# A new hand-out of places: the same 1,848 steps of a recurrence and four attention experts in another order

## The chip, the core and the metric

The kernel runs on one core of a Trainium2 chip. The engines are TensorE (PE in the profile, its weight loads PEld), VectorE (DVE), ScalarE (ACT), GpSimd (POOL) and SyncE (SP), which starts the DMAs. The metric is the device time of one execution in microseconds (us); of three executions of the kernel before, the median is 308.04 us (307.08 to 311.17).

## The reference

Two stages, with B=4 batches, H=8 heads, S=768 steps, D=48, and then E=4 experts with 64 columns each.

```python
for t in range(S):                       # stage 1: a recurrence over steps, per batch and head
    cur = einsum(u * k[t], v[t])
    y[t] = einsum(r[t], state + cur)
    state = w[t] * state + einsum(k[t], v[t])
x = y as (B, S, H*D)                     # (4, 768, 384)
logits = x @ w_gate                      # stage 2: the 2 best of 4 experts for each row
for e in range(4):
    q, k, v = x @ wq[e], x @ wk[e], x @ wv[e]
    a = softmax(causal(0.125 * q @ k.T))
    out += gate[e] * (a @ v @ wo[e])
```

## The kernel before

The 768 steps of a batch are cut into two halves of six chunks of 64 steps, so there are eight units (batch, half). Each unit goes through the recurrence (`rwkv`) and then through the experts (`moe`); different units overlap.

**Recurrence.** The heads go in pairs, two pairs together (in the first unit pair by pair). DVE scans the decays of a chunk (L623 backward, L630 forward), and keys and receptances are multiplied with the results (L632, L634, L636, L638, on DVE or POOL). PE turns the scaled keys (L257 as one 128x128 product, L261 as two products on quarters of the array: the first when the product ahead used the whole array), makes each chunk's state increment (L445) and the products inside a chunk (L686), whose copy is masked (L693). DVE carries the state from chunk to chunk, one step an instruction (L468, first step L470 or L472, last step L464). PE then adds both parts of the output into one bank (L399, L401: the output products), and DVE adds the bonus term (L412 in the first unit, where PE sums the bonus with L570). PE turns the sums into columns for the experts.

**Experts.** Projections (L772 and L811 in the first unit in plain fp32, L779 and L817 after it), scores (L881), row maximum and mask on DVE (L892), exponential on ACT (L897), transposes (L257, L261), a times v (L929), gates (L966, L978), output projection (L1000), copy and store.

**What sets the order.** Nothing is scheduled while the kernel runs or is built: every step was given a number when it was planned, and the table `ORDER` lists the numbers with the letter of an engine (A is ACT, V DVE, P PE, G POOL, S SP). The lists of the engines are followed one by one:

```python
listed = [(letters[x[0]], int(x[1:])) for x in ORDER.split()]
for e, n in listed:
    o = ops[n]                     # also picks the buffer and the bank that o gets
...
    o["fn"](o["how"])              # writes the instructions of o
    if e == "PE":  pe = ...        # the last product so far
    elif e == "SP" and pe is not None:
        tc.add_manual_dep(own, pe.name, ...)   # "pace": a DMA waits for it
```

So an entry's place sets its place in its engine's queue, and for a DMA also the product after which it may start. A step whose plan allows two engines goes to the one whose letter it has.

**Warming products.** 94 steps (numbers 8 to 101, line L1054) multiply a constant tile by itself and write a bank that nobody reads; a step that isn't in the table isn't made. They need only the constant and a free bank.

```python
for i in range(WARM[0] + WARM[1]):
    plan.add("warm", {"PE": 216}, lambda e, w=w: nc.tensor.matmul(w()[:, 0:512], wz[:, 0:128], wz, ...), [], [w], ...)
```

Other lines: L329 and L330 (`masks3`) make the mask inside a chunk, L333 (`masks2`) the causal mask, L563 the bonus products, L578 the products of two decays, L643, L656, L664 and L666 the bonus of later units, L267 and L265 copies on DVE and ACT.

Of the kernel before, what the change touches and what calls it, by code (L numbers as in the profile page):

```python
# [1095 lines left out]
A0 V4 S113 V123 V124 A1 V126 S114 S115 S116 A5 A125 V120 G128 S6 S117 P79 S176 P53 P28 P9 P68 P88 P10 G129 V3 S177 P94  # L1096
S180 S119 P21 V127 P86 V130 P34 P90 V145 V131 P133 P100 V146 V148 V149 P50 P20 G142 G150 V152 P27 G151 V147 V153 S243
S244 V2 P57 G184 A134 P135 V185 A136 S118 V137 S245 V187 P31 V138 P143 A144 P155 A156 P121 S178 V188 P47 P157 G154
A158 G206 V159 A122 G132 S246 V160 V139 V161 P165 S102 A168 G169 V207 V162 A208 S7 S107 V140 V163 V209 V141 V210 A251
A186 P164 V166 G250 V252 A274 V253 A268 P51 P173 V174 P170 S249 G255 G257 V171 P74 V254 S179 P237 A238 A295 V203 V181  # L1100
V211 P265 P204 V213 G212 V189 A266 P182 A183 V214 V191 A205 P216 G190 V192 G193 V256 A217 S287 G258 S288 A105 G106
P267 P218 A219 G294 V220 V269 V221 V222 P194 A195 P225 S289 P196 V227 A197 V198 G299 A108 V223 V199 V200 G300 V224
V201 S340 P226 V229 A103 V202 G104 V270 V275 P231 V276 V232 A215 P234 V235 V277 S248 S247 V271 G347 V278 V279 S293
V272 V273 S290 V296 V297 S342 V298 V348 P916 P241 P239 P280 V281 V259 V260 A240 A242 G301 S341 G302 V261 V263 G353
G352 V349 S291 G303 G304 V283 P912 P913 S384 G391 S386 A312 A318 S385 P920 P921 P922 A923 P914 A915 G354 P967 P917
P918 V350 V351 G397 A264 A919 P968 P969 P309 A970 A310 P937 P946 V938 A939 V940 A941 A262 V949 A950 V947 A948 P311
V319 V320 S343 V313 V314 V315 V316 P955 V956 A957 V317 V321 V322 V323 P944 A945 V305 V307 S344 A392 V393 V394 A306
P971 V958 P972 P973 A974 A308 P924 P925 P926 P324 P285 S292 P928 P929 V325 A959 P930 P951 V327 P953 S387 G355 V286
A927 S346 P960 A931 V932 A954 V396 A952 A961 V356 G357 G933 P362 P962 S438 P975 V976 A363 V978 A977 G398 V395 P331
S437 A332 G109 A963 A360 S439 V333 G444 P329 V330 P364 P942 V371 V943 P984 P337 V985 A365 P334 A335 A338 S345 V358  # L1110
A359 S388 V372 V373 A986 G399 S110 V336 V374 A361 S535 V339 A979 V375 V376 S390 V366 V987 A988 V367 V368 S480 V369
S482 V370 S481 P964 P965 P966 A1005 P377 V378 V380 V400 P1033 P1034 P1041 P1035 V448 V401 P1042 P1043 P1037 A1036
A1044 P980 P991 A981 A992 A934 V935 P1038 V402 A111 P1039 A1040 V404 S441 P993 P989 A990 G449 P982 A983 G405 V996 V994
P1058 A997 V1061 G936 P406 A407 V1059 V445 A995 V1007 V1008 G1009 V446 P1067 P1000 A1001 G1010 V1070 A1062 V1068 P408
A415 A409 V410 A403 V416 V411 G112 P1049 P998 A1060 A999 V417 V418 V419 V412 V413 V414 P1050 P1051 A1052 P1045 P1046
P1047 V447 P1011 P1091 P1092 A1012 A1071 G487 S440 A1048 G452 V420 P1093 A1094 G450 P1013 V1014 A1015 P421 V422 P1074
A1075 V424 P1076 V1077 P1065 A1066 A1069 A1078 V1079 A1080 G1016 P382 V383 V451 V488 V1053 V453 V491 V456 S533 G492
G1054 S532 G543 V454 V489 G539 P1002 S389 A461 P1003 P1004 A1006 S534 S484 S442 P458 A459 P1072 A1073 P1081 A1082
P1095 P1096 P1097 A1098 A467 P1017 V1018 A1019 G1020 P460 V462 V468 V463 V469 V464 V470 P473 V474 A476 P1083 A1084
A1055 A457 V471 V465 P1099 V1102 A1103 V1100 A1101 V472 A455 V466 P426 V427 A510 V490 S486 S443 P1108 G494 V1111 V1109  # L1120
A1112 V1056 V493 V495 V540 V496 S577 S483 G1057 V497 G477 G545 P1021 P1063 P434 P1104 A435 S575 A1064 P1022 A1023
S1024 G582 V541 S576 P1029 P1030 A1105 A504 P1025 P1026 A1027 S1028 A1031 S1032 A1110 P1117 V1118 P501 A502 V499 S536
G544 V1120 P1085 P428 A429 P431 V430 A432 V433 V436 P1086 P503 V505 V511 V512 V506 V513 V507 A1119 A1121 A498 V1134
V542 V514 V508 V515 V509 P478 V479 S485 G546 S629 P516 V517 V583 V587 A519 V547 S627 V586 V548 V549 V1135 S538 G520
G1136 V551 S628 A500 G588 S578 V584 G1137 P1087 G639 P1088 P1089 P1090 A1132 P1106 A1107 P1115 A1116 P553 A554 S579
P1160 P1161 P1162 A1163 V1164 P1165 P1166 P1167 A552 P555 V556 V557 G634 V558 V562 V559 V563 V564 V565 V560 A1168
V1169 V566 P568 A571 V569 V567 V561 A550 P521 V522 P1222 P1223 P1224 S580 A1225 V1226 V590 S537 V585 V589 P1113 P523
A524 V525 A1114 G572 P1124 S768 S670 P1217 P1218 G591 G638 P1138 A1125 S672 A1139 P1219 A1220 V1221 P529 A530 P1122
P596 A1123 V531 P1140 V1141 P1187 P1196 A597 P526 A1142 A527 P1205 V1190 V1188 V1197 A594 V1199 A1200 V528 A595 A1198
V635 G1143 A592 G677 A593 A1191 S671 G681 G640 A1189 P611 V612 P598 V605 V599 V600 V601 V602 V1206 S631 S630 V606 V636  # L1130
V607 V608 V609 V610 G682 A1207 P573 V574 V603 V604 P1126 V614 A651 V637 V641 S581 V678 V642 P1127 P1128 P1129 P1130
S633 P1131 A657 S722 A1133 P1303 P1304 P1305 V679 P1170 P1171 V643 P1295 P1172 P1299 A1306 P648 P1192 A1193 P1203
A1204 P1300 P1301 A649 A1173 A1302 V680 P1296 P1297 A1298 A644 V1307 G1308 P1144 A645 S723 G683 G729 V646 A647 V1145
A1146 A1309 P650 G1147 V1208 V658 V659 S674 S673 P663 A1209 V652 V660 V666 V664 V653 V654 P616 V617 P1178 P1179 P1180
P1290 P1291 P1345 V685 P1292 V686 A1181 P1346 A1293 A700 V1310 V687 P1347 A1348 P1174 V1349 P1175 P1176 V655 G684 A689
G690 S726 A1177 P621 P624 A694 S765 V661 V662 P1210 V656 G1311 A625 A622 S632 V1294 V626 A1211 V623 P1350 P1351 P1352
V1182 V730 G1183 A1353 V1354 A688 P1285 P1286 P1287 A1288 V1289 P1156 P1157 G733 G735 S823 P1194 A1195 A1158 P1227
V731 V1228 G772 P618 V1230 S724 G734 P1201 V1202 S767 P691 A619 P1236 P1245 V620 V1239 A1231 A692 V1237 P1212 A1213
V1248 P1234 A1235 V1246 A1247 S766 P693 S1159 V701 V695 V702 V696 V703 V697 V698 V699 V704 A1229 A1184 V1185 G1186
P668 V705 S675 V669 V732 A1238 A1249 A1240 V1259 G737 S725 G736 V1260 G1261 G738 G1262 P1214 P1215 P1216 P1250 A1251  # L1140
S819 P1252 G777 A1253 P1312 V1315 S817 G776 G829 S676 P1243 P1241 A1257 A1242 A1244 A1316 S818 V1313 A1314 P1148 P1149
# [126 lines left out]
```

## Time and profile before

| | us |
|---|---|
| three executions | 308.04, 307.08, 311.17 |
| the profiled execution | 308.01 |
| its span, first to last instruction | 306.1 |
| PE busy in the span | 295.6 |
| DVE busy | 248.1 |
| ACT, POOL busy | 222.0, 155.3 |
| mean granted clock of TensorE | 0.989 |

The span is what the trace shows; 1.91 us of the profiled execution lie around it. A matmul's end is modelled, so that products that follow each other closely overlap in the trace, and a short wait can hide in a busy time. The granted clock is told as a share of 2.4 GHz, so 0.50 is 1.2 GHz.

### The profile page before, as it was taken

The page shows a single profiled execution, that of the slowest core. Times are in us where ns is not written, and L with a number is a line of the kernel's source. Part 1 is how long each engine was busy: PE and PEld are TensorE (multiplying, and loading weights), DVE is VectorE, ACT ScalarE, POOL GpSimd, SP SyncE. Part 2 cuts the span into 40 slices and gives each one's busy share as a digit, 9 for nine tenths or more (in the row PEclk, how much of TensorE's full clock was granted, in tenths as well). Part 3 has the DMA queues.
Part 4 walks back from the last instruction along what each step waited for, and adds up shares of the span by engine and source line. Part 5 has one row for each costly group of instructions (what it writes and reads, how often), then busy time and mean ns, then how long its engine had stood idle before and what let it go on. Part 6 is the DMA issues. An engine that isn't in the chain of part 4 may idle for free.

```text
span 306.1 us, 12703 instructions
## 1 busy us (share of the span) xinstructions
PE 295.6 (97%) x5216; PEld 245.0 (80%) x5216; DVE 248.1 (81%) x703; ACT 222.0 (73%) x688; POOL 155.3 (51%) x247
## 2 busy tenths in 40 slices
PE   7879999899999999999999999999999999999995
PEld 2669669778886897999789778898889977898784
DVE  5987999989999999989898997978587644687652
ACT  4336399988999889889899867464788656649852
POOL 4848597928556548267787769634211101210510
PEclk9995999999999999999999999999999999999999
DMA  7976785881649763656671573010100000000212
GB/s 227 359 277 216 255 277 167 292 300 43 212 134 329 222 208 117 218 163 207 206 232 77 173 271 107 6 41 24 51 28 2 0 28 28 2 26 2 79 62 94
DMA packets 20073, 44.09 MB, mean 144 GB/s; under 512 B 2352, under 2 KB 10032, under 8 KB 20016
## 3 DMA queue, kind: packets, MB, share of 16 engines
q1 hardware_dynamic: 20016, 43.29, 42.8%
q8 instruction: 41, 0.67, 0.9%
q14 instruction: 16, 0.13, 0.1%
HBM read 38.56 MB, written 4.72 MB: 141 GB/s over the span
## 4 chain that ended last, share of the span: by engine, by line
PE 93%; DVE 3%; issue 1%; DMA 1%; SPq 0%; ACT 0%; DVEq 0%; ACTq 0%
PE ps L779 16%; PE ps L929 13%; PE ps L881 12%; PE ps L1000 9%; PE ps L261 9%; PE ps L817 8%; PE ps L686 5%; PE ps L257 4%; PE ps L399 4%; PE ps L401 4%; PE ps L445 3%; PE ps L772 3%; PE ps L811 1%; DMA lt<-in_wkr_dram 1%; PE ps L978 1%
## 5 line engine op out<-in xcount | busy, mean ns | idle before, releaser
L897 ACT ACTIVATE a<-a,mx 128x128 f32<-128x128 f32 (+5 forms) x96 | 63.8, 667 | 10.0 <-DVE mx L892 9.6
L892 DVE CUSTOM_DVE_ANT_0 a<-ps,causal 128x256 f32<-128x256 f32 (+5 forms) x96 | 56.4, 619 | 12.2 <-PE ps L881 10.8
L265 ACT COPY AT<-ps 128x512 f32<-128x512 f32 (+5 forms) x74 | 38.6, 546 | 10.1 <-PE ps L261 7.9
L929 PE MATMUL ps<-AT,v_sb 128*64 128x384 f32 (+2 forms) x308 | 40.4, 405 | 0.1
L468 DVE CUSTOM_DVE_ANT_0 ys<-ps,ys,suf 112x48 f32<-112x48 f32 x144 | 33.4, 262 | 3.2 <-PE ps L445 0.4
L929 PEld LDWEIGHTS ps<-AT,v_sb 128*64 128x64 f32 x308 | 20.0, 136 | 16.5 <-issue 12.2
L664 ACT ACTIVATE xn<-nat,rk 128x48 f32<-128x48 f32 x126 | 30.5, 326 | 2.0 <-DVE rk L656 1.9
L779 PE MATMUL ps<-xh,wh_qk 128*128 128x384 f32 x84 | 30.4, 362 | 0.0
L881 PE MATMUL ps<-K,Q 64*128 64x384 f32 (+4 forms) x160 | 30.2, 415 | 0.0
L779 PE MATMUL ps<-xl,wh_qk 128*128 128x384 f32 x84 | 28.4, 338 | 0.1
L779 PE MATMUL ps<-xh,wl_qk 128*128 128x384 f32 x84 | 28.3, 336 | 0.0
L989 POOL TENSOR_TENSOR yl<-yr,yh 128x384 fp32r<-128x384 f32 x13 | 13.1, 1010 | 27.5 <-ACT yh L988 26.3
L399 PE MATMUL ps<-vy,am 64*64 64x48 f32 x768 | 25.8, 225 | 1.3 <-issue 1.3
L261 PEld LDWEIGHTS ps<-ident,a 64*128 64x128 f32 x560 | 23.1, 138 | 4.4 <-issue 1.6
L261 PE MATMUL ps<-ident,a 64*128 64x64 f32 x560 | 26.3, 225 | 0.1
L401 PE MATMUL ps<-ys,pre 48*64 48x48 f32 x704 | 25.5, 224 | 0.0
L636 POOL TENSOR_TENSOR kt<-lt,suf 128x768 f32<-128x768 f32 x13 | 21.9, 1685 | 6.3 <-DVE kr L643 3.5
L401 PEld LDWEIGHTS ps<-ys,pre 48*64 48x64 f32 x704 | 22.9, 138 | 2.2 <-DVE wend L464 1.1
L399 PEld LDWEIGHTS ps<-vy,am 64*64 64x64 f32 x768 | 23.5, 139 | 0.1
L638 POOL TENSOR_TENSOR pre<-lt,w 128x768 f32<-128x768 f32 x11 | 18.6, 1690 | 9.6 <-DVE w L630 5.4
L686 PE MATMUL ps<-pre,kt 48*64 48x64 f32 x768 | 18.3, 227 | 1.4 <-issue 0.7
L693 DVE TENSOR_TENSOR am<-ps,dec_mask 64x384 f32<-64x384 f32 (+1 forms) x33 | 18.2, 552 | 1.4 <-PE ps L686 1.0
(173 smaller groups left out, 823.2 us busy)
## 6 DMA issues: line engine op xcount, KB each, us to landing
lt<-in_wkr_dram SPq DMA_DIRECT2D x28, 384.0 KB, 4.4
kr<-in_nat_dram SPq DMA_DIRECT2D x14, 576.0 KB, 4.2
lt<-in_wkr_dram SPq DMA_DIRECT2D x14, 397.0 KB, 4.4
nat<-in_nat_dram SPq DMA_DIRECT2D x16, 288.0 KB, 3.9
vy<-in_vY_dram SPq DMA_DIRECT2D x32, 144.0 KB, 3.7
out_dram<-ob SPq DMA_DIRECT2D x24, 192.0 KB, 1.9
lt<-in_wkr_dram SPq DMA_DIRECT2D x3, 583.0 KB, 5.8
w_qk<-in_wqk_dram SPq DMA_DIRECT2D x1, 768.0 KB, 8.0
```

The lines of the kernel that those rows point to most:

```text
L261: nc.tensor.transpose(o()[:, h * 512 + i * 64:h * 512 + i * 64 + 64], src[r], ident[r, r])
L265: nc.scalar.copy(o, i)
L399: nc.tensor.matmul(to, am()[k, c, :], vy()[k, c, :], start=zero and x == 0, stop=i == 2 and x == len(group) - 1)
L401: nc.tensor.matmul(to, pre()[r, c, :], ys()[r, c, :], start=i == x == 0, stop=False)
L468: nc.vector._custom_dve(TENSOR_TENSOR_REDUCE_ADD_MIN, out=new, in0=inc, in1=old, s0=3.0e38, s1=by)
L664: nc.scalar.mul(to[:, i, h, :], v()[:, i, h, :], rk()[:, i, h:h + 1])
L686: nc.tensor.matmul(apss[x]()[half(h if first else h ^ x), c * C:(c + 1) * C], kt()[r, c, :], pre()[r, c, :], start=True, stop=True)
L779: nc.tensor.matmul(pp()[:, 0:384], w[:, qk, k, cs], x()[:, k, :], start=(k == j == 0), stop=(k == j == 2))
L881: nc.tensor.matmul(spv(x)[:, h, :], q_()[p, t], flat(k_())[p, o], start=j == 0, stop=j == len(terms) - 1)
L892: nc.vector.tensor_tensor_reduce(out=a()[:, 0:n].rearrange("p (a n) -> p a n", a=np_), in0=spv(x), in1=causal[:, S - n:S].rearrange("p (a ...
L897: plan.add("exp", {"ACT": t_exp(n)}, lambda e, x=x, y=y, mx=mx, a=a: nc.scalar.activation(a()[:, 0:n], a()[:, 0:n], AF.Exp, bias=mx(), sca ...
L929: nc.tensor.matmul(yp()[e * 64:e * 64 + 64, lo:hi], v_sb()[:, j, ep * 128 + e * 64:ep * 128 + e * 64 + 64], at, start=(j == 0), stop=(j == ...
```

## The change

Only the table `ORDER` is another one. It lists 1,848 steps, where the one before has 1,847. 83 steps change the engine: 34 from ACT to DVE, 31 from DVE to ACT, 9 from POOL to DVE, 6 from DVE to POOL, 2 from POOL to ACT and 1 from ACT to POOL. Warming products: 22 in place of 21. The rows of the product lines stay in number, but for the transposes, of which 22 of quarters (L261) become 11 of the whole array (L257), because the product ahead of them is another one.

```diff
 ORDER = """
-A0 V4 S113 V123 V124 A1 V126 S114 S115 S116 A5 A125 V120 G128 S6 S117 P79 S176 P53 P28 P9 P68 P88 P10 G129 V3 S177 P94
...
+V4 S113 V123 A0 V2 A5 V3 S115 S114 S116 V124 V120 S6 V126 G128 P92 V127 G129 V130 S117 P54 S176 P53 P68 V145 V146 V148
...
 """
```

**PE, first pair of heads.** Before: the last state increments, all products inside the chunks, one warming product, and the output products:

```order
L445 MATMUL ps<-nat_129,kts_212 48x48 x12
L686 MATMUL ps<-pre_155,kt_150 64x64 x24
L1054 LDWEIGHTS causal
L1054 MATMUL ps<-causal 128x512
L401 MATMUL ps<-ys_234,pre_155 64x48 x2
L399 MATMUL ps<-vy_145,am_260 64x48 x4
```

Now (the lines left out are three more warming products):

```order
L445 MATMUL ps<-nat_134,kts_204 48x48 x12
L686 MATMUL ps<-pre_143,kt_132 64x64 x12
L1054 LDWEIGHTS causal
L1054 MATMUL ps<-causal 128x512
...
L686 MATMUL ps<-pre_143,kt_132 64x64 x12
L401 MATMUL ps<-ys_227,pre_143 64x48 x2
```

The products of the two heads' chunks are parted, and four warming products stand between them. Ahead of the first keys' transposes stand eight warming products where there were twelve; up to the end of the output products there are 18 in place of 20, and nothing else is more or less there.

**PE, behind the output products of the first pair.** Before:

```order
L399 MATMUL ps<-vy_197,am_289 64x48 x4
L1054 LDWEIGHTS causal
L1054 MATMUL ps<-causal 128x512
L257 MATMUL ps<-ident,xn_323 128x128 x3
L257 MATMUL ps<-ident,kt_350 128x128 x6
L570 MATMUL ps<-u_t,kr_363 128x2 x6
L257 MATMUL ps<-ident,kt_376 128x128 x3
```

Now (left out: two more warming products):

```order
L399 MATMUL ps<-vy_192,am_284 64x48 x4
L1054 LDWEIGHTS causal
L1054 MATMUL ps<-causal 128x512
...
L257 MATMUL ps<-ident,xn_316 128x128 x3
L257 MATMUL ps<-ident,kt_319 128x128 x6
L1054 LDWEIGHTS causal
L1054 MATMUL ps<-causal 128x512
L570 MATMUL ps<-u_t,kr_349 128x2 x6
```

Three warming products stand where one stood, and a fourth ahead of the bonus sums. The first projection step (L772) goes ahead of the second pair's last products inside chunks, and the next unit's products inside chunks (L686, 24 rows) go ahead of two transposes of the sums.

**DVE, the start.** Before, the mask (L329, L330) stands behind both heads' scans; the rows here are the first after the constants:

```order
L578 TENSOR_TENSOR w_114<-lt_66 128x199
L623 SCALAR_TENSOR_TENSOR ps<-w_114,ps 128x198
L628 RECIPROCAL ps<-ps 128x6
L563 TENSOR_TENSOR kr_125<-lt_66 128x2x192
L333 TENSOR_SCALAR causal<-d_78 128x128
L630 SCALAR_TENSOR_TENSOR ps<-w_114,ps 128x198
...
L329 TENSOR_SCALAR dec_mask<-d_78 64x64
```

Now:

```order
L578 TENSOR_TENSOR w_112<-lt_66 128x199
L329 TENSOR_SCALAR dec_mask<-d_78 64x64
L330 TENSOR_SCALAR dec_mask<-d_78 64x64
L333 TENSOR_SCALAR causal<-d_78 128x128
L623 SCALAR_TENSOR_TENSOR ps<-w_112,ps 128x198
L563 TENSOR_TENSOR kr_124<-lt_66 128x2x192
L628 RECIPROCAL ps<-ps 128x6
```

Both masks now stand ahead of the bonus product (L563), which needs two loads. Further on, the next unit's receptance product (L634, 128x384) leaves DVE for POOL, and six state steps (L468) of the next unit that stood behind the second pair's additions (L412) stand ahead of them. The loads keep their set; the weights of the projections (`w_qk`) start four loads earlier.

## Rows read from the trace of the kernel before

**Rows 1.** The page, busy time of each engine, share, instructions.

```profile
PE 295.6 (97%) x5216; PEld 245.0 (80%) x5216; DVE 248.1 (81%) x703; ACT 222.0 (73%) x688; POOL 155.3 (51%) x247
```

**Rows 2.** Stretches: us, length, each engine's busy us (instructions), granted clock, DMA share, GB/s.

```profile
6.60:23.66 17.06, 13.25 (x302) 10.47 (x303) 15.71 (x43) 5.88 (x19) 11.35 (x16) 1.00 0.87 310
23.66:30.48 6.82, 6.64 (x168) 6.27 (x168) 4.77 (x19) 4.00 (x12) 5.62 (x5) 0.50 0.75 241
30.48:298.00 267.52, 265.93 (x4709) 222.80 (x4711) 222.62 (x629) 207.13 (x647) 135.53 (x214) 1.00 0.40 131
```

**Rows 3.** PE's waits up to 31 us: line, for whom, us in total, times, longest.

```profile
PE ps L399 <- issue: 1.3, 1, 1.3
PE ps L1054 <- DVE ys L468: 0.8, 1, 0.8
PE ps L257 <- DVE kt L636: 0.7, 1, 0.7
```

**Rows 4.** The chain that ended last: start, us, what.

```profile
7.38 0.55 PE ps L257 x3
...
17.29 1.28 issue
18.57 0.21 PE ps L399
...
24.16 1.36 PE ps L686 x21
...
31.29 0.66 PE ps L257 x6
31.94 0.86 PE ps L686 x48
...
35.60 3.87 PE ps L772 x12
...
113.38 1.64 PE ps L257 x15
...
249.06 1.03 PE ps L261 x30
```

**Rows 5.** DVE's waits from 3.4 to 31 us, columns as in Rows 3.

```profile
DVE am L693 <- PE ps L686: 0.8, 2, 0.7
```

**Rows 6.** Two stretches of DVE, columns as in Rows 2.

```profile
3.41:24.09 20.68, 16.87 (x314) 11.69 (x312) 18.35 (x50) 7.28 (x22) 11.81 (x16) 0.99 0.87 299
24.09:30.94 6.85, 6.67 (x164) 6.15 (x162) 4.82 (x19) 3.60 (x10) 6.08 (x6) 0.53 0.74 238
```

**Rows 7.** Instructions of DVE in order of time: start, us, engine, line.

```profile
5.49 0.56 DVE L563 TENSOR_TENSOR kr<-lt 128x384 f32<-128x384 f32 x1 [0.81 <-DMA lt<-in_wkr_dram]
...
10.63 0.67 DVE L329 TENSOR_SCALAR dec_mask<-d 64x64 f32<-64x64 f32 x1
11.32 0.55 DVE L330 TENSOR_SCALAR dec_mask<-d 64x64 f32<-64x64 f32 x1
...
18.81 0.46 DVE L412 TENSOR_TENSOR xn<-ps,kr 128x288 f32<-128x288 f32 x1 [0.86 <-PE ps L399]
...
23.52 0.55 DVE L634 TENSOR_TENSOR lt<-lt 128x384 f32<-128x384 f32 x1
...
24.09 0.92 DVE L468 CUSTOM_DVE_ANT_0 ys<-ps,ys,suf 112x48 f32<-112x48 f32 x4
...
30.48 0.46 DVE L412 TENSOR_TENSOR xn<-ps,kr 128x288 f32<-128x288 f32 x1 [0.82 <-PE ps L399]
```

**Rows 8.** Warming products in order of time, columns as in Rows 7.

```profile
1.42 5.30 PE L1054 MATMUL ps<-causal 128*128 128x512 bf16 x12 [1.42 <-POOL causal L285]
...
7.77 1.24 PE L1054 MATMUL ps<-causal 128*128 128x512 bf16 x5
```

**Rows 9.** The page, DMA queue, kind: packets, MB, share.

```profile
q8 instruction: 41, 0.67, 0.9%
```

**Rows 10.** A long stretch of the middle, columns as in Rows 2.

```profile
38.25:130.05 91.80, 90.71 (x1986) 74.43 (x1988) 87.03 (x246) 82.69 (x287) 57.65 (x74) 1.00 0.64 210
```

More of the change, by code (lines that the diff above doesn't have):

```diff
@@ L1101 @@
[L1101 to L1105, printed above, removed]
@@ new lines @@
+V199 V224 V200 A215 G347 V270 V201 V271 V202 P916 V279 A108 V272 S289 G300 G299 P226 V229 V273 P231 V232 P234 V235
+S247 V296 A318 S290 S249 V297 V298 V348 P280 V281 V283 S342 V259 V260 V261 G301 V263 G302 G353 S341 S292 V349 V350
+A312 V351 V392 P912 S291 S384 P239 S386 P241 P967 A240 S385 G352 P917 A242 P968 P969 P920 P918 A970 A919 A262 P913
+P921 P922 A923 P914 A915 P928 P929 P309 A310 P937 P946 V940 A941 V938 V949 A939 A950 A264 V947 S387 P955 A948 V958
+A959 P944 A945 V956 A957 V303 G304 P311 V319 V313 V320 V321 V314 V322 V315 V323 V316 V307 V305 S344 A308 V317 A306
@@ new lines @@
+P971 P930 V931 G354 V397 P924 G391 G396 P972 P973 P285 V286 S293 S390 G355 S343 S439 P324 P925 P962 S437 P953 V327
+V325 A963 A974 P951 A954 P926 V393 V394 P362 A927 A952 P960 P331 P942 A363 S438 V932 V356 G357 G933 P975 V976 V978
+P329 P364 A961 V395 A332 V330 A943 V333 P984 V987 A360 G399 V358 S346 G109 V371 S388 V985 G398 P337 A338 V339 P334
+A335 A365 V336 A977 V366 A979 S110 V372 S482 S345 A359 A988 A934 A361 A986 V367 V368 V373 V369 P964 P965 P966 V374
+V375 S480 P377 P1037 P1038 V378 P1039 P982 P1033 V380 A983 P1041 P1034 P1035 P1042 A1005 P1043 P980 A1036 A1040 A981
@@ new lines @@
+V1589 S1411 P1606 P1607 P1608 A1609 P814 A815 V816 V1610 A1590 P1510 P1511 P1512 A1514 P1575 V1576 P808 A809 V810
+P1593 A1594 P1611 V1614 V1612 P1584 V1585 P811 A812 V813 A1613 P1591 V1592 A1615 P1797 P1798 P1799 P1802 A1800 P1803
+P1804 P1525 V1526 V1801 A1805 P1620 P1616 A1527 G1528 V1623 A1624 P1729 P1730 P1731 A1732 V1621 A1617 V1733 P1629
+V1632 A1622 P1582 A1633 V1630 A1631 A1583 P1533 P1534 P1672 V1535 S1536 V1646 V1647 V1648 P1529 P1530 A1531 S1532
+P1677 P1678 P1679 V1806 A1680 P1673 P1674 V1681 V1675 V1676 G1649 P1650 A1651 P1595 P1596 P1597 P1598 P1599 P1600
@@ new lines @@
+A1644 P1627 P1699 V1700 A1628 P1618 A1619 P1636 P1625 V1702 A1637 A1701 P1708 P1717 P1634 V1626 V1709 P1704 V1718
+A1719 A1703 V1720 A1635 A1710 A1721 P1537 P1538 P1734 P1735 P1736 P1652 V1711 A1712 V1539 P1713 V1653 A1654 V1705
+V1655 V1737 V1738 P1638 P1639 P1640 P1641 P1642 P1643 P1724 A1645 V1714 A1725 P1722 V1723 P1739 P1748 P1715 V1742
+V1740 P1757 A1716 P1706 S1540 P1656 V1751 A1752 P1682 V1657 V1760 P1683 P1690 A1658 V1659 A1707 P1686 P1684 A1685
+V1749 P1691 P1692 A1743 V1693 P1687 A1750 P1688 P1660 A1741 P1661 P1755 A1756 V1689 V1694 A1662 G1695 V1758 A1759
@@ new lines @@
+P1746 A1747 P1726 P1727 P1728 A1769 P1744 P1762 A1696 A1745 V1763 V1697 A1761 G1698 G1771 P1824 V1827 P1753 A1754
+V1825 P1833 A1826 P1764 A1765 V1836 A1837 V1772 V1834 P1862 P1863 P1815 P1864 P1857 P1858 A1835 V1865 V1866 G1773
+P1859 V1860 V1861 G1774 P1775 A1776 S1663 A1828 P1816 P1817 P1842 V1818 V1843 P1831 V1845 P1766 A1832 P1767 P1768
+A1770 P1829 A1830 P1838 P1867 P1840 A1839 P1807 A1844 V1870 P1811 P1812 V1868 A1841 P1781 V1782 P1777 A1871 A1846
+P1808 P1809 V1810 V1778 P1813 A1814 P1876 V1819 V1877 P1849 A1869 P1847 G1820 A1878 A1821 A1850 V1879 A1880 V1822
@@ new lines @@
+G1823 V1848 V1906 V1907 P1664 P1665 A1666 P1668 V1908 P1669 A1779 P1885 G1780 V1670 A1783 G1784 V1886 A1887 G1909
+P1881 V1882 V1888 A1889 V1929 V1930 S1671 G1931 P1851 P1852 P1853 P1854 P1855 P1856 A1905 P1883 A1884 P1874 P1872
+P1890 V1875 A1891 P1892 S1667 V1873 P1910 A1893 P1785 P1786 V1911 P1793 P1916 G1932 P1789 P1794 P1933 A1934 P1790
+P1939 A1940 P1935 V1936 P1912 V1913 A1914 V1915 A1795 A1937 V1938 S1796 A1787 S1788 P1899 P1900 V1791 S1792 P1894
+P1901 P1902 P1895 P1903 P1904 P1896 P1897 P1898 V1941 A1942 V1943 A1917 V1918 A1919 V1920 P1944 P1945 A1946 S1947
@@ L1184 @@
+P1921 P1922 A1923 S1924 P1925 P1926 A1927 S1928
 """
```

138 lines of the change are left out of this document (56 added, 82 removed).

## The prediction, made before the change was timed

> **What bounds the kernel now.** The page comes first: PE is busy 295.6 us of the 306.1 us span, 97% [rows 1]. A new order makes no product shorter, so it can win only where PE waits, where it runs at the lower clock, or where it does work that nobody needs. The stretches by granted clock say where that is [rows 2]: from 30.48 to 298 PE is busy 265.93 of 267.52, which leaves 1.59 us; from 6.60 to 23.66 it is busy only 13.25 of 17.06; and from 23.66 to 30.48 it is busy nearly all the time, at a granted clock of 0.50, which is 1.2 GHz. The price of that is in the chain: 21 products inside chunks take 1.36 us at 24.16, 48 of them 0.86 us at 31.94 [rows 4]. Ahead of the fall PE had waited three times for 0.7 to 1.3 us [rows 3] and had made few products; no gap was longer than 1.28 us [rows 4].
>
> Then the other side of the first 31 us: who holds PE up there? DVE is busy 18.35 of the 20.68 us from 3.41 to 24.09, so this stretch is DVE's chain of scans and state steps, with PE waiting for it. In the next, from 24.09 to the end of the first unit's last addition at 30.94 (30.48 and 0.46 [rows 7]), DVE is busy 4.82 of 6.85 [rows 6] and its long waits are for PE, 0.8 and 0.82 [rows 5, 7]: there the slow PE holds up DVE. So the start can give something, the long rest 1.59 us at most by what the trace shows as idle.
>
> **The change, part by part.** The sum is made against the profiled execution, 308.01 us, 0.03 under the median of the three.
>
> *1. DVE up to 24.09.* Three things leave this stretch.
> The masks (0.67 and 0.55 us [rows 7]) go to where DVE waits 0.81 us for the load of the bonus product [rows 7]. Their work stays, the wait goes: between 0, should the load come later than now, and 0.81. I take 0.81, since the same two loads stand at the same place of the queue, only in turned order.
> The receptance product of 0.55 us at 23.52 [rows 7] goes to POOL, which is busy 11.81 of these 20.68 us [rows 6]; its taker is PE's products inside chunks for the next unit, some 5 us later, so POOL hides it. A key and a receptance product trade engines: nothing.
> DVE's first wait for the output products (0.86 at 18.81 [rows 7]) is the shadow of the gap of 1.28 us at 17.29, which stands ahead of one product of L399, the last of its group [rows 4]. PE waited for "issue" there, so for no engine and no load. I read it as a wait for the instructions themselves: 41 packets of instructions make 0.67 MB [rows 9], one for each 255 or so of PE's 10,432 instructions [rows 1], and the DMA share is 0.87 here [rows 2]. Such a gap belongs to a place in PE's stream. Ahead of the group's end there are now 18 warming products in place of 20, so the group ends two products before that place, and the gap falls among the warming products behind it, where nobody waits. So 0.86 goes; the other end is 0.
> The Trainium skill, in "Runtime: NRT & Kernel Launch" (Instruction fetch mechanics), says that the sequencer streams blocks of 256 instructions and that crossing into the next is mostly hidden. The size agrees with 41 packets; by "hidden" the gap would have another cause and would stay, and the sum would come out 0.86 us higher.
> What DVE meets when its own waits are gone are the short handoffs: 20.68 less 18.35 less 0.81 and 0.86 is 0.66 us now; I add 0.4, between 0 and 0.66.
> So the state steps that begin at 24.09 begin at 24.09 - 0.81 - 0.86 - 0.55 + 0.4 = 22.27.
>
> *2. DVE from there to the last addition.* If the clock stays at 1.00, PE's 6.64 us of busy time here [rows 2] are about 3.3, and the projection step that is moved in adds 0.65 (3.87 us for 12 products, two a step [rows 4]): 4.0 us, less than DVE needs. DVE keeps its 4.82 and gets six state steps that stood behind the additions and one first step that was ACT's, 7 at 0.23 (0.92 for four [rows 7]), 1.6: 6.4, and 0.4 of handoffs again: 6.8. The additions end at 29.1 in place of 30.94, with 1.6 us of later DVE work already done, so that DVE is ahead by 3.4 us then.
> Does the clock stay? The four warming products more between the chunk products and three behind the group come where the trace has waits of 0.8 and 1.28 us [rows 3, 4], and one more stands ahead of the bonus sums. At the full clock each is about 0.22 us (five in 1.24 us with the last one's end [rows 8]), together about 1.3 us more of dense products in the 8 us ahead of 23.66. I hold that likelier than not; nothing in this trace shows how little more is enough.
>
> *3. PE from there on.* The last output products must end before the last addition starts, at 29.1 - 0.46 = 28.6. Then come the next unit's products inside chunks, 0.86, one projection step, 0.65, and the transposes of the sums, 0.66 [rows 4]: 30.8. Before, the same steps are done when the 48 products that start at 31.94 are through, at 32.80, and one projection step more is made, at 33.45 (the other step moved is in both sums). PE is ahead by 33.45 - 30.8 = 2.65. From here it is busy without a pause in the trace before, so this lead reaches the end if DVE can follow, and DVE's lead is the larger one.
>
> *4. Costs and the rest.* 22 transposes of quarters become 11 of the whole array: 11 x 0.109 (1.64 for 15) less 22 x 0.034 (1.03 for 30) [rows 4] is 0.45 us on PE, where nothing hides it. The eight warming products at the start cost nothing: PE waits for the first keys then. The 83 steps that change engines add none to PE; DVE, ACT and POOL have room on the mean [rows 1]. I take 0 for the 1.59 us of idle time after 30.48: an order can lose there as well as win, down to 1.59 less, up to rival 3. At the end the same products stand behind the same casts: 0.
>
> The sum: 308.01 - 2.65 + 0.45 = 305.8 us.
>
> **The rivals.** *1. The clock falls all the same.* Then the stretch at 0.50 comes back, term 2 loses what DVE no longer waits (2.03 less 0.4), and the time is 305.8 + 1.6 = 307.4. For it: before the fall the stretch was three quarters busy, and most of what the change adds is warming, 0.22 us a piece. Against it: seven or eight such pieces stand where there were gaps. It is also the case in which the change does not do what it says. The Trainium skill, in "TensorE: Matmul & The Clock Gate" (What's actually happening), says that the watch over PE's activity runs freely and doesn't start with the kernel; by this the same order would keep its clock in one execution and lose it in another, and times of 305.8 and 307.4 would both be seen. One trace can't show that; the three times before spread over 4.1 us. Chance 0.2.
>
> *2. Slower: the clock comes late.* The first run of warming products is eight in place of twelve. At 5.30 us for twelve [rows 8] they end near 4.9, and PE then waits for the first keys until about 7.4 (at 7.38 now [rows 4], after a wait of 0.7 [rows 3]). If PE is still at 1.2 GHz when the keys come, and stays there for as long as the one slow stretch of the trace, 6.82 us [rows 2], its work there doubles: 13.25 of 17.06 busy [rows 2] makes 5.3 us in 6.82, so 5.3 more, less the 1.5 of idle time that it can use, and the warming products stand ahead of what DVE waits for. DVE's chain then comes 3.8 us later: 309.6. It is decided by the clock when the first keys are turned. Against it: in the trace before, full clock is there from 6.60, and eight products may be enough. Chance 0.1.
>
> *3. The lead is given back.* From 38 to 130 us DVE is busy 87.03 of 91.80 us beside PE's 90.71 [rows 10]; a new order can put a wait anywhere, and gaps for "issue" fall elsewhere when instructions move. Three more gaps of 0.7 us are 2.1: 307.9. For it: two engines near their limit and 83 steps moved between them. Against it: DVE's lead of 3.4. Chance 0.18.
>
> *4. More is won.* The 1.59 us idle after 30.48 go too, and the handoffs of 0.4: 303.8. Chance 0.1.
>
> **How the numbers follow.** The forecast, 305.8, has 0.42. By its own bounds it reaches from 305.8 - 0.8 (no handoffs at all) to 305.8 + 1.7 (load and instruction gap stay): 305.0 to 307.5. With rivals 1, 3 and most of 4 the range is 303.2 to 309.2; left out are rival 2, the low end of rival 4 and what nobody thought of. A measurement of this kernel tells some 2% from no change, 6.2 us: under 301.9 or over 314.2. No case reaches either; I leave 0.05 for faster, for waits that hide in PE's modelled busy time, 0.03 for slower, and 0.92 for within 2%.
>
> **What would show it.** Right: a granted clock of 1.00 without a break from about 7 us to the end; DVE's wait for the bonus load gone; a gap for "issue" near 17 to 18 us that stands among warming products, and no wait of the first additions for it; state steps of the second pair from about 22.3; the first unit's last addition over at 29.1; PE about 2.6 us ahead when the long run of first projections (L772) starts. Wrong: a stretch at 0.50 behind 20 us (rival 1) or one that reaches past 7.4 us (rival 2); PE idle much over 1.6 us from there to the last 8 us (rival 3). If both leads are there at 31 us and the time is not, step 3 is the one that failed.

## The result and the profile after

The changed kernel takes 311.05 us (median of 22 executions, 308.49 to 312.91) against 309.10 us for 22 of the kernel before: ratio 1.008 [1.006, 1.011]. In a later batch (e5 below) it was 311.09 and 1.005 [1.002, 1.009]. So it is slower by 0.5 to 0.8%, where 305.8 us and a gain were forecast, and it lies outside the range of 303.2 to 309.2. A ratio leaves out, on both sides, executions more than 1.5% over the fastest of their kernel, while medians and means are over all. The execution that was profiled took 312.14 us; its span is 310.3. It is 1.1 us over its median and the one profiled before is 1.1 under its own, so the two traces lie 4.1 us apart where the medians lie 1.95 apart: they show the loss at about twice its usual size.

The page of the changed kernel, busy time of each engine, answers to [rows 1]: PE has 2.5 us more of it, with ten products fewer.

```profile
PE 298.1 (96%) x5206; PEld 247.3 (80%) x5206; DVE 249.4 (80%) x708; ACT 221.4 (71%) x676; POOL 149.8 (48%) x242
```

Its stretches between the changes of the granted clock, columns as in [rows 2]:

```profile
3.41:14.10 10.69, 7.80 (x49) 4.55 (x47) 7.58 (x24) 2.02 (x6) 4.39 (x7) 1.00 0.67 228
14.10:24.34 10.24, 7.71 (x185) 5.78 (x185) 9.37 (x23) 3.69 (x12) 6.33 (x7) 1.00 0.92 281
24.34:31.16 6.82, 6.82 (x132) 6.16 (x131) 3.78 (x13) 2.85 (x8) 5.56 (x6) 0.50 0.41 132
31.16:302.00 270.84, 269.02 (x4810) 226.07 (x4810) 225.91 (x644) 208.12 (x642) 131.20 (x211) 1.00 0.42 134
```

The clock falls at 24.34 for 6.82 us, as long as before and 0.7 later. The 1.00 of the first row is not to be believed: the first record of the clock is at 14.10, and what stood ahead of it is read from durations. Products in order of time, columns as in [rows 8]:

```profile
1.42 3.59 PE L1054 MATMUL ps<-causal 128*128 128x512 bf16 x8 [1.42 <-POOL causal L285]
7.90 0.90 PE L257 MATMUL ps<-ident,kt 128*128 128x128 f32 x3 [2.89 <-DVE kt L636]
8.60 1.28 PE L570 MATMUL ps<-u_t,kr 128*128 128x2 f32 x6
9.74 1.87 PE L1054 MATMUL ps<-causal 128*128 128x512 bf16 x4
11.54 0.73 PE L445 MATMUL ps<-nat,kts 64*48 64x48 f32 x24
```

Three transposes of keys take 0.90 us; before they took 0.55 [rows 4]. Four warming products take 1.87, where five took 1.24 [rows 8]. So PE is at 1.2 GHz until 14.10, with the six bonus sums (L570) and four warming products in front of the state increments (L445).

Then the loads. The queue of SP, start, us, what, first of the kernel before, then of the changed one (lt are the keys, receptances and decays of a pair, vy the values):

```profile
5.06 1.03 SPq L274 DMA_DIRECT2D vy<-in_vY_dram  x2
8.82 1.39 SPq L274 DMA_DIRECT2D lt<-in_wkr_dram  x2
...
11.38 2.11 SPq L274 DMA_DIRECT2D nat<-in_nat_dram  x2
13.59 0.38 SPq L274 DMA_DIRECT2D w_qk<-in_wqk_dram  x1
```

```profile
8.84 4.33 SPq L274 DMA_DIRECT2D vy<-in_vY_dram  x2
13.26 2.21 SPq L274 DMA_DIRECT2D lt<-in_wkr_dram  x2
16.13 0.33 SPq L274 DMA_DIRECT2D w_qk<-in_wqk_dram  x1
...
18.87 0.86 SPq L274 DMA_DIRECT2D nat<-in_nat_dram  x2
```

Every row starts 2.5 to 7.5 us later, also that of w_qk, although w_qk stands four loads earlier in the list. (The two rows of vy share one load; the other of the first row comes at 20.31 now.) A load waits for the last product listed ahead of it, and for its buffer; in the new table those are other products, and here they are late products, too. A late start is not always a late landing: by the trace w_qk lands 0.5 us later than before (22.09 for 21.63), the second of the two lt 5.6 (19.84 for 14.29) and the first nat 5.5 (24.50 for 18.98). The chain of waits shows where that ends, columns as in [rows 4]:

```profile
8.81 1.07 PE ps L570 x6
9.88 1.73 PE ps L1054 x4
...
15.14 4.69 DMA lt<-in_wkr_dram
...
19.97 0.94 POOL lt L632
...
20.98 2.12 POOL kt L636
23.14 0.87 PE ps L257 x6
...
24.23 2.14 PE ps L570 x12
...
36.46 0.65 PE ps L257 x6
```

The load lands at 19.83, POOL makes the keys from it (L632, then L636), and PE stands still for 2.3 us until 23.14. Some 1.5 us of that are the load's: what L636 needs of DVE (L267) was there at 19.37, and L636 began at 20.98. Another 0.4 is L636 itself, 2.12 us here for 1.67 before, when it began at 17.47 and waited for DVE alone:

```profile
17.47 1.67 POOL L636 TENSOR_TENSOR kt<-lt,suf 128x768 f32<-128x768 f32 x1 [1.44 <-DVE suf L623]
```

DVE of the changed kernel in order of time, columns as in [rows 7]:

```profile
3.69 0.18 DVE L329 TENSOR_SCALAR dec_mask<-d 64x64 f32<-64x64 f32 x1
3.88 0.19 DVE L330 TENSOR_SCALAR dec_mask<-d 64x64 f32<-64x64 f32 x1
...
5.91 0.56 DVE L563 TENSOR_TENSOR kr<-lt 128x384 f32<-128x384 f32 x1 [1.11 <-DMA lt<-in_wkr_dram]
...
19.23 0.14 DVE L267 COPY suf<-ps 128x6 f32<-128x6 f32 x1
19.29 0.45 DVE L412 TENSOR_TENSOR xn<-ps,kr 128x288 f32<-128x288 f32 x1
...
21.03 2.48 DVE L563 TENSOR_TENSOR kr<-lt 128x384 f32<-128x384 f32 x2
...
28.39 0.27 DVE L468 CUSTOM_DVE_ANT_0 ys<-ps,ys,suf 112x48 f32<-112x48 f32 x1 [2.50 <-ACT wh_qk L354]
...
35.04 0.46 DVE L412 TENSOR_TENSOR xn<-ps,kr 128x288 f32<-128x288 f32 x1 [0.39 <-PE ps L399]
```

State steps of the second pair begin at 28.39 (24.09 before [rows 7]) and the first unit's additions end at 35.50 (30.94). From there on little is lost: PE's waits of the changed kernel from 31.16 to 300 us, columns as in [rows 3], are few.

```profile
PE ps L686 <- issue: 0.7, 1, 0.7
PE ps L257 <- POOL kt L636: 0.3, 1, 0.3
```

The set of steps that the prediction followed is through at 37.11 (36.46 and 0.65), 3.66 later than 33.45 before; the whole execution is 4.13 later, and the difference, 0.47, is close to what the transposes of the whole array were priced at (0.45), though no run prices them apart. So in this pair of executions the loss is made in the first 31 us, nearly all of it.

### The profile page after: what moved, and what is told of

Its sections match the earlier page's. It is cut to its first block, busy times and chain, and to the rows that moved or that the text cites. A ratio compares the mean times of both kernels' runs of the same rounds, so it can differ in the third digit from the quotient of the medians.

```text
span 310.3 us, 12665 instructions
## 1 busy us (share of the span) xinstructions
PE 298.1 (96%) x5206; PEld 247.3 (80%) x5206; DVE 249.4 (80%) x708; ACT 221.4 (71%) x676; POOL 149.8 (48%) x242
## 4 chain that ended last, share of the span: by engine, by line
PE 89%; DVE 4%; DMA 3%; POOL 2%; issue 1%; SPq 0%; ACT 0%; POOLq 0%; DVEq 0%
PE ps L779 15%; PE ps L929 13%; PE ps L881 12%; PE ps L1000 9%; PE ps L261 9%; PE ps L817 8%; PE ps L257 5%; PE ps L686 4%; PE ps L445 3%; PE ps L399 3%; PE ps L401 3%; DMA lt<-in_wkr_dram 3%; PE ps L772 2%; PE ps L570 1%; POOL kt L636 1%; PE ps L978 1%
## 5 line engine op out<-in xcount | busy, mean ns | idle before, releaser
L897 ACT ACTIVATE a<-a,mx 128x512 f32<-128x512 f32 (+5 forms) x96 | 63.9, 667 | 8.0 <-DVE mx L892 7.7
L265 ACT COPY AT<-ps 128x128 f32<-128x128 f32 (+5 forms) x76 | 40.2, 544 | 8.1 <-PE ps L261 6.0
L468 DVE CUSTOM_DVE_ANT_0 ys<-ps,ys,suf 112x48 f32<-112x48 f32 x144 | 32.5, 260 | 8.6 <-ACT wh_qk L354 2.5
L261 PEld LDWEIGHTS ps<-ident,a 64*128 64x128 f32 x544 | 22.9, 138 | 5.3 <-issue 2.2
L261 PE MATMUL ps<-ident,a 64*128 64x64 f32 x544 | 26.6, 226 | 0.0
L399 PE MATMUL ps<-vy,am 64*64 64x48 f32 x768 | 24.7, 219 | 0.0
L401 PE MATMUL ps<-ys,pre 48*64 48x48 f32 x704 | 24.3, 219 | 0.0
L636 POOL TENSOR_TENSOR kt<-lt,suf 128x768 f32<-128x768 f32 x12 | 20.7, 1724 | 6.7 <-PE ps L811 2.3
L401 PEld LDWEIGHTS ps<-ys,pre 48*64 48x64 f32 x704 | 21.7, 134 | 1.8 <-DVE ys L468 0.8
L989 POOL TENSOR_TENSOR yl<-yr,yh 128x384 fp32r<-128x384 f32 x12 | 12.1, 1016 | 22.5 <-ACT yh L988 16.1
L638 POOL TENSOR_TENSOR pre<-lt,w 128x768 f32<-128x768 f32 x10 | 16.9, 1686 | 9.0 <-DVE ys L468 2.8
L841 POOL TENSOR_TENSOR ge<-v_sb,m 128x12 f32<-128x12 f32 x8 | 1.7, 210 | 39.2 <-DVE c L837 39.2
L265 ACT COPY kts<-ps 128x768 f32<-128x768 f32 (+1 forms) x18 | 13.2, 732 | 9.5 <-PE ps L257 7.6
```

Source lines behind the costliest of these rows:

```text
L261: nc.tensor.transpose(o()[:, h * 512 + i * 64:h * 512 + i * 64 + 64], src[r], ident[r, r])
L265: nc.scalar.copy(o, i)
L399: nc.tensor.matmul(to, am()[k, c, :], vy()[k, c, :], start=zero and x == 0, stop=i == 2 and x == len(group) - 1)
L401: nc.tensor.matmul(to, pre()[r, c, :], ys()[r, c, :], start=i == x == 0, stop=False)
L468: nc.vector._custom_dve(TENSOR_TENSOR_REDUCE_ADD_MIN, out=new, in0=inc, in1=old, s0=3.0e38, s1=by)
L897: plan.add("exp", {"ACT": t_exp(n)}, lambda e, x=x, y=y, mx=mx, a=a: nc.scalar.activation(a()[:, 0:n], a()[:, 0:n], AF.Exp, bias=mx(), sca ...
```

## The experiments

Four theories stood against each other. **1:** the clock comes late, because PE has eight warming products at the start, not twelve. **2:** the loads of the next pairs and of the next unit are late, because each waits for a later product. **3:** the loss lies in the rest, behind 31 us. **4:** the new order of DVE's steps in the start holds up PE. All sixteen kernels differ from the two in the table alone. The times of a kernel spread widely from execution to execution (those of the kernel before from 305.0 to 315.2 us), so each was timed 12 times (e7, e11 and e16 6 times), beside 29 to 35 executions of the kernel before on the same chip; these have a mean of 309.4 us.

| kernel | median | mean | ratio to before |
|---|---|---|---|
| e5, the changed kernel again | 311.09 | 311.1 | 1.005 [1.002, 1.009] |
| e1, changed + 12 warming products | 310.75 | 310.5 | 1.003 [0.999, 1.007] |
| e3, changed + early loads | 309.32 | 310.2 | 1.006 [1.001, 1.010] |
| e4, changed + both | 309.70 | 310.2 | 0.999 [0.995, 1.003] |
| e8, e4 + all loads early | 309.36 | 309.4 | 0.999 [0.994, 1.003] |
| e16, e8 + six state steps late | 311.92 | 312.1 | 1.011 [1.007, 1.016] |
| e2, before with 8 warming products | 308.84 | 309.1 | 1.000 [0.996, 1.004] |
| e6, old start, new rest | 307.69 | 308.3 | 0.996 [0.991, 1.000] |
| e9, e6 again | 309.39 | 308.8 | 0.995 [0.991, 1.000] |
| e10, e6 + loads partly late | 309.17 | 308.9 | 1.002 [0.998, 1.006] |
| e13, e6 + late loads | 309.44 | 309.8 | 1.002 [0.999, 1.005] |
| e12, e6 + new warming products | 309.12 | 309.4 | 1.003 [0.999, 1.007] |
| e14, e6 + late loads + new warming | 311.48 | 312.0 | 1.010 [1.006, 1.014] |
| e15, e6 + seven more warming products | 309.03 | 308.7 | 0.998 [0.995, 1.002] |
| e11, e6 + DVE's new order | 319.36 | 319.3 | 1.029 [1.023, 1.035] |
| e7, new start, old rest | 324.36 | 324.9 | 1.048 [1.042, 1.053] |

**Warming products and loads taken back in the changed kernel: e1, e3, e4, e8.** e1 puts four more at the start:

```diff
-... P32 P52 P133 A134 ...
+... P32 P52 P8 P9 P11 P12 P133 A134 ...
```

> The changed kernel with four more warming products in its first run, twelve as in the kernel before. Theory 1 (the clock comes late because eight are too few: in the changed kernel the durations of PE's products show 1.2 GHz until 14.10 us, and the first increments are at 11.5 in place of 8.9): the keys' transposes take about 0.55 us in place of 0.90, the increments start near 9, and most of the 3.6 us of PE's lag at the long run of first projections goes: about 308 us, 3 under the changed kernel's 311. Theory 2 (what is late are the loads of the next unit, since each waits for the product listed ahead of it): the loads stand behind the same products, which come some 2 us earlier, so about half goes: 309 to 310. Theory 3 (the loss lies behind 31 us): 311.

e3 lists four loads earlier (V153 moves too, since it frees their buffer), and e4 does both:

```diff
-... P52 P133 A134 S119 P121 G151 P35 V152 P81 ... P31 V153 ... S118 A122 S243 ... S244 ...
+... P52 S119 P133 A134 P121 G151 P35 V152 V153 S118 S243 S244 P81 ... P31 ...
```

> The changed kernel with four loads of the next unit listed earlier: the two decay loads and one more (steps S118, S243, S244) directly behind the last user of their buffer, so behind the first increments' predecessors and no longer behind the products inside chunks, and the load S119 ahead of the first keys' transposes in place of behind them. Still eight warming products. Theory 1: the first clock stays late, and the time stays within 0.7 us of the changed kernel, 310.4 to 311. Theory 2: the decay loads land near 17 us in place of 19.8, POOL's product of the decays (line 632) and PE's transposes behind it no longer wait 2.3 us, and the time falls by 2 to 3, to about 308.5. Theory 3: 311.

> Both edits together: twelve warming products at the start, and the four loads earlier. Theory 1: as with the twelve products alone, about 308. Theory 2: about 307 to 308, under each edit alone. If both lags add up, this gives the lead that the prediction saw: 306 to 307. Theory 3: 311.

e8 is e4 with the loads S245, S178, S246, S102, S7 and S107 earlier as well (behind S244, P121, P157 and, the last three, P165).

> The changed kernel with twelve warming products at the start and every load of the first 25 us listed as early as in the kernel before or nearly so: beside the four of the earlier run also the third decay load, both loads of keys by rows (nat), the bonus rows and both blocks of projection weights. Theory 2: the 2.2 us that PE waits for nat in the run with four loads moved go as well, and the time is 307 to 308, under the kernel before. Theory 3: 309.5 to 311, no better than with four loads moved. If loads crowd each other: PE or DVE waits for a first load instead, and the time is 310 or more.

Each edit alone is not told from no change: e1 and e3 are 0.4 and 0.8 us under the mean of the changed kernel's 34 executions (310.9), with standard errors of 0.5 and 0.6. For e4 the two measures disagree: its ratio is that of the kernel before, but its mean, 310.2, is e3's. e8 is back by both: 309.4 where e5, beside it on the same chip, has 311.1. So with twelve at the start and all loads early the loss is gone. All loads early with eight was not run; from this side it stays open whether e8 needs both. Why e3 gains little its trace says: the decay loads come in time there, yet POOL's keys start at 20.83 in place of 20.98, because DVE's part, behind products at 1.2 GHz, is as late as the load was.

```profile
20.83 1.67 POOL L636 TENSOR_TENSOR kt<-lt,suf 128x768 f32<-128x768 f32 x1 [0.73 <-DVE suf L267]
```

An early load also uncovers the next: the chains of e4 and of e8 run over another load in its place.

```profile
15.86 8.48 DMA nat<-in_nat_dram
```

```profile
14.53 4.79 DMA w_qk<-in_wqk_dram
```

**The kernel before with eight: e2.** Its table with four products fewer at the start:

```diff
-... S119 P21 V127 P86 V130 P34 P90 V145 ...
+... S119 V127 V130 V145 ...
```

> The kernel before with eight warming products in its first run in place of twelve, all else as it was. Theory 1: PE is at 1.2 GHz when the first keys come, the first increments move from 8.9 to about 11, and the kernel ends 2 to 3 us later than before, about 311 to 312. Theory 2: its loads stand ahead of most of these products, so it stays within 0.5 us of the kernel before, 309. Theory 3: the same, 309.

No difference (in its trace the first keys were turned in 0.55 us): eight at the start don't hurt by themselves, where the loads and the other warming products stand as before. Theory 1 as it was put falls.

**The changed kernel again: e5.**

> The changed kernel itself once more, so that the other kernels of this round can be set against it on the same chip, and to see whether the late first clock (14.10 us) belongs to the order or to the execution. By theory 1 it belongs to the order (eight warming products): full clock comes late again. By the other theories nothing hangs on it. Time 311, from 309.5 to 311.5.

Here the clock came otherwise. Stretches between its records, and the first products:

```profile
5.58:8.99 3.41, 1.42 (x11) 1.19 (x12) 3.04 (x8) 0.48 (x1) 1.95 (x3) 1.00 0.98 349
8.99:12.41 3.42, 3.42 (x35) 2.01 (x33) 3.07 (x9) 0.58 (x4) 2.46 (x5) 0.50 0.50 192
12.41:22.65 10.24, 8.23 (x189) 6.15 (x189) 9.39 (x24) 4.26 (x12) 5.88 (x7) 1.00 0.92 281
22.65:32.89 10.24, 10.07 (x197) 8.29 (x198) 6.77 (x27) 4.78 (x16) 7.32 (x8) 0.50 0.60 185
```

```profile
7.57 0.55 PE L257 MATMUL ps<-ident,kt 128*128 128x128 f32 x3 [2.55 <-DVE kt L636]
...
9.98 0.73 PE L445 MATMUL ps<-nat,kts 64*48 64x48 f32 x24
```

The same program, and full clock first at 5.58 us in place of 14.10: the keys are turned at 2.4 GHz, the increments again at 1.2. The Trainium skill, in "TensorE: Matmul & The Clock Gate" (What's actually happening), says that the watch over PE runs freely and does not start with the kernel; these two traces agree. By the rows, the late first clock is not the order's alone, and this execution took 311.02 us without it: full clock was lost again from 8.99 to 12.41 and from 22.65 to 32.89. The load that held up POOL in the first trace landed at 18.14 here, 0.4 us behind DVE's part, and cost little.

**Where the loss lies: e6, e7, e9.** The table of one kernel up to the first unit's last addition (V235), and from there the other's entries that have not been listed yet, in its order, without its warming products of the start.

> The order of the kernel before up to the first unit's last addition, the changed order from there on. If the loss lies in the start (theory 2, or theory 1): about 309, like the kernel before, or 308 if the new rest is better. Theory 3 (the loss lies behind 31 us): about 311, like the changed kernel.

> The other half: the changed order up to the first unit's last addition, the order before from there on. If the loss lies in the start: about 311. Theory 3: about 309.

> The best kernel so far, the start of the kernel before with the changed rest, once more beside three kernels that each put one part of the changed start back into it. It was 307.69 beside 309.75 for the kernel before. If that is real, its ratio to the kernel before is again 0.993 to 0.998; if it was chance, 0.998 to 1.003.

Old start with new rest is no slower than the kernel before, twice, and if anything 0.5% faster; theory 3 falls. It has the best mean of all, 308.6 over 24. e7 can't be read as the other half: two pieces that don't fit make a third kernel, with 27 us at a granted clock of 0.50. Its stretch:

```profile
23.34:50.65 27.31, 22.89 (x318) 17.01 (x318) 16.24 (x43) 8.46 (x27) 19.46 (x18) 0.50 0.71 244
```

**Parts of the changed start put into e6: e10 to e14.** e10 and e13 move loads, e12 the warming products, e14 both. At the first keys (P133) and the increments (P135), e13 and e12 against e6 read:

```diff
-... S177 P94 S180 S119 P21 ... P133 P100 ... V153 S243 S244 V2 ... A134 P135 V185 A136 S118 ...
+... P94 S177 P21 ... P133 S119 P100 ... V153 V2 ... A134 P135 S118 S243 V185 A136 ...
```

```diff
-... P34 P90 V145 V131 P133 P100 ... P50 P20 ... P27 ... P57 ... A134 P135 V185 ... P165 ...
+... V145 V131 P133 P35 P81 P94 P100 ... A134 P135 P31 P83 V185 ... P165 P74 P10 P14 P99 ...
```

> Start of the kernel before, changed rest, but every load of the first 30 us stands behind the same product as in the changed kernel, that is later; warming products and the lists of PE, DVE, ACT and POOL as in the start before. Theory 2 (late loads): slower than the kernel with the old start by 1.5 to 3, about 309.5 to 311. Theory 1 (clock) and theory 4 (the order of DVE's steps): no slower, 307.7.

In e10 some loads stood a few products too early (the decay loads went out at 9.75), which is why e13 was made.

> Start of the kernel before, changed rest, and now each load of the first 25 us truly behind the same product as in the changed kernel: the first value load behind the first keys, the next value load and the first decay load behind the first increments, the second decay load behind the second increments, the projection weights behind the first products inside chunks. (In the run with late loads before this one some of them still stood a few products earlier.) Warming products as in the start before. Kernels with the old start took 308.6 on the mean of 24 runs, the changed kernel 311.0 of 34. Theory 2 alone: 310.5 to 311. Theory 1 alone: 308.6. Both with a share: about 309.5.

> Start of the kernel before, changed rest, but the warming products stand where the changed kernel has them: 8 at the start in place of 12, 4 behind the first keys, 2, 4 and 3 behind the next groups, 1 ahead of the second pair's products; all else as in the start before. Theory 1 (the clock comes late): slower by 1.5 to 3, 309.2 to 310.7. Theory 2: within 0.7 of the kernel with the old start. By the prediction's second term (more warming in the gaps holds the clock): faster by up to 1.6, 306.

> The same with the warming products as in the changed kernel too (8 at the start, the others in the gaps): loads and warming of the changed kernel, lists of DVE, ACT, POOL and of PE's products as in the start before. If late loads and a late clock are all of the loss: 311. If the order of the steps has a share of its own: 309.5 to 310. If a late clock makes the loads later still (they wait for products at 1.2 GHz), this is slower than the sum of both single effects over 308.6, about 0.9 for the warming and what the loads alone show.

Against e6 and e9 (308.6, 0.995) late loads alone come to 309.8 and 1.002, the warming alone to 309.4 and 1.003, both to 312.0 and 1.010, which is the changed kernel or a little more. The single ones are near the edge of what these runs tell (the means are 1.2 and 0.9 us over that of the 24, each with a standard error of 0.6, the medians 0.4 and 0.1 over 309.06), so their shares stay open. That the two together make the whole loss is shown by e14, which has all else of the start as before, and from the other side by e8. How the late loads take part is not seen: in the traces of e13 and e14 no load but the first stands in the chain of the first 36 us, and that of e14 is of its slowest execution (316.37), which also lost 1.88 us to a gap for "issue" at 31.98. What the warming does is seen in e12, PE's products and two stretches, beside the same of e6:

```profile
7.47 0.90 PE L257 MATMUL ps<-ident,kt 128*128 128x128 f32 x3 [2.46 <-DVE kt L636]
8.17 1.91 PE L1054 MATMUL ps<-causal 128*128 128x512 bf16 x4
10.01 0.73 PE L445 MATMUL ps<-nat,kts 64*48 64x48 f32 x24
...
18.32 1.23 PE L686 MATMUL ps<-pre,kt 48*64 48x64 f32 x18
```

```profile
7.55 0.55 PE L257 MATMUL ps<-ident,kt 128*128 128x128 f32 x3 [1.74 <-DVE kt L636]
7.94 1.24 PE L1054 MATMUL ps<-causal 128*128 128x512 bf16 x5
9.11 0.48 PE L445 MATMUL ps<-nat,kts 64*48 64x48 f32 x24
```

```profile
1.40:20.37 18.97, 16.49 (x160) 10.52 (x163) 11.21 (x37) 5.19 (x16) 9.80 (x20) 1.00 0.84 273
```

```profile
1.40:20.37 18.97, 14.86 (x235) 9.56 (x236) 15.65 (x45) 6.58 (x22) 11.48 (x21) 1.00 0.94 330
```

In e12 the first record of full clock is at 20.37, and it never falls again; up to there PE makes 160 products for e6's 235. Its span is 309.4 for 304.0. In most of its executions (7 of 12) the mean granted clock is 0.996 or more, and those take 309.6: the mean counts from the first record, so a clock that comes late looks like one that never fell. How often the first keys meet 1.2 GHz, the traces of all kernels tell: with eight warming products at the start, their transposes take 0.90 us in 5 of 7 profiled executions, with twelve in 1 of 11 (that of e16), and else 0.55. In four of the five the first record of full clock comes behind them, at 13.10 to 20.51; in e3 and e16 it had come at 4.32 and 4.20 and the clock fell again at 7.73 and 7.61, just ahead of them.

**DVE's order: e11, e16.** e11 gives e6 the list of DVE's steps from the changed start; e16 takes six state steps (V277, V278, V271, V279, V272, V273) in e8 to behind V235.

> Start of the kernel before, changed rest, but DVE's steps in the first 30 us stand in the order of the changed kernel (masks ahead of the bonus product, six state steps of the next unit ahead of the last additions, two first state steps on DVE); loads, warming products and PE's list as before. Theory 4 (this order holds up PE): 309 to 310. Theories 1 and 2: within 0.7 of the kernel with the old start, 307 to 308.4; by the prediction's first term it would be faster by up to 1.4, 306.3.

> The changed kernel with 12 warming products at the start and all loads early, as run before (309.4), and now also the six state steps of the next unit behind the first unit's last additions, where the kernel before has them, in place of ahead of them. Theory 4 (these 1.4 us of DVE's work stand in the way of the additions and so of PE): faster by 0.7 to 1.4, about 308.3. By the prediction (the same work is done in either place, and DVE has time): no change, 309 to 309.8.

Both came out worse than any theory had it, e11 10.7 us over e6 and e9, e16 2.7 over e8, and neither tells what DVE's order costs. In e16's trace PE is at 0.50 from 7.61 for 13.65 us. In e11 five warming products wait 1.31 us, in front of the increments, until DVE has read the bank that they write, and in that trace PE is at 0.50 for 17.07 and for 13.66 us:

```profile
9.26 2.32 PE L1054 MATMUL ps<-causal 128*128 128x512 bf16 x5 [1.31 <-DVE pre L638]
```

Theory 4 stays open, and isn't needed: e14 has the old lists and the whole loss.

**Holding the clock: e15.** Seven more in the gaps of e6:

```diff
-... A134 P135 ... V161 P165 ... V174 P170 ... V211 P265 ...
+... A134 P135 P8 ... V161 P165 P11 P12 P13 ... V174 P170 P14 P15 ... V211 P265 P16 ...
```

> Start of the kernel before with its 12 warming products at the start and all its others, and seven more in the gaps where the changed kernel has them (1 behind the first increments, 3 ahead of the products inside chunks, 2 behind the first output products, 1 ahead of the second pair's products), changed rest. Theory 1 (time at 1.2 GHz is what most differs): the clock comes by 7 us and stays, in nearly all executions, and the time is 306 to 307, the best of all. If the added products only take PE's time: 309 to 310.

They hold it: granted clock 1.00 from 4.64 us to 305.0 in the profiled execution, 0.989 or more in all 12. The time is still 308.7, not the 306 to 307 that theory 1 had. In that execution some of what was won went to a gap for "issue" that came to stand in front of the second pair's output products; the chain:

```profile
27.80 1.46 issue
```

## Why the prediction was wrong

- **Step 4, "the eight warming products at the start cost nothing: PE waits for the first keys then"**, is one of the two that failed. PE does wait then, but at 1.2 GHz afterwards, and the bonus sums and warming products that now stand in front of the increments take 2.8 us at that clock (1.07 and 1.73). It is rival 2, which had 0.1 and gave 309.6; the profile before showed full clock at 6.60 behind twelve, and that was read as room to spare. Alone, in e12, it costs 0.9 us with an error of 0.6.
- **The loads were not priced at all.** The prediction said that the two loads of the bonus product stand at the same place, and went no further, though what sets a load's start is the product ahead of it in the table, and all of those moved. In the profiled execution one of them made 1.5 of the 2.3 us of waiting ahead of 23.14. The late clock delays the very products that the loads wait for; that fits with both together costing more (2.4 us in the changed kernel, 3.4 in e14, over e6 and e9) than either alone, but it is argued: no run takes it further apart.
- **Step 1** said 22.27 for the second pair's state steps; they began at 28.39, behind the two lags above. Its parts: the masks took 0.37 us in place of 1.22, better than thought; the wait for the load did not go but grew from 0.81 to 1.11, since the load itself landed later in this execution; no gap for "issue" shows up to 31 us (its place in PE's stream has moved among the warming products, see the last section), and the first additions at 19.29 wait for nothing, as forecast.
- **Step 2**, "does the clock stay? I hold that likelier than not": it fell at 24.34, behind the wait for the late keys. Rival 1's price fits: it took 1.6 us for 6.82, or 0.23 us for each us at 1.2 GHz. In the 122 executions of the kernel before that were timed beside the experiments, the 16 with a mean clock of 0.996 or more (mean 0.999) took 307.6 us, the 35 from 0.97 to 0.98 (mean 0.976) took 311.1. A clock lower by 0.0235 is 14.4 us of 306 at 1.2 GHz; 3.5 us over 14.4 is 0.24. That the slow clock makes these executions slow, and not only goes with them, is argued: e15 held the clock and won nothing.
- **Step 3 and rival 3**: what is lost or won at 31 us does reach the end in this pair of executions (3.66 of 4.13; the rest is close to the 0.45 of the transposes). The step was right; it carried a loss.
- The sum was made against an execution 1.4 us under the later mean, so it started too low by that much. The spread of the three times (307.1 to 311.2) was set beside the clock in rival 1 only; in the 122 executions times and mean clocks go together (correlation -0.76).

## What to carry to other kernels

Where a DMA is tied to a place in another engine's list, a new order of that engine is a new order of the loads: write down for each load which instruction releases it, before and after. Where an engine's clock depends on what it did, the first microseconds decide by the durations of like products, not by the mean granted clock, and one trace shows one case out of several. Put back two suspected causes singly and together, from both kernels: here only the pair moved the time clearly beyond its error.

## What the hardware showed

**Gaps for "issue" sit at fixed places in PE's stream.** Count all of PE's records from the start: products, weight loads and waits for semaphores. In the kernel before, the gap of 1.28 us stands behind record 449 (17.07 us), the 1.46 us of e15 behind record 961, and in 17 of 18 traces 0.6 to 1.8 us pass from start to start behind record 1982 to 1985 (some records can be missing): 512 and twice 512 apart. All 40 waits of PE for "issue" of 0.2 us or more in the 18 traces stand within two records of 449 plus a multiple of 256, whatever product is there. That supports the prediction's reading of instruction fetch, one packet for each 255 or so. In the changed kernel record 449 is a warming product, at 19.23; the next one waits 0.18 us for DVE, and a gap beside that doesn't show. The Trainium skill, in "Runtime: NRT & Kernel Launch" (Instruction fetch mechanics), speaks of blocks of 256 instructions and calls the crossing into the next mostly hidden. The traces agree: each has some 41 such places, and one to four show; but those that show took up to 1.88 us (e14).

**DVE and POOL slow each other, by the look of two rows.** The masks took 0.67 and 0.55 us at 10.63 [rows 7] and 0.18 and 0.19 at 3.69; two bonus products (L563) took 2.48 us at 21.03, where one takes 0.56. POOL was at work beside the slow ones (its L636 ran from 20.98 for 2.12 us, and takes 1.67 in the kernel before). No run tested it.
